# Scores of ten head pairs from q and k in two float32r parts, epsilon carried by the rows past the keys, and a new order of work

## The chip, the cores and the metric

The kernel runs on one core of one Trainium2 chip. The metric is the device time of one execution in microseconds (us). The kernel before took 669.44 us, the median of three runs (669.27 to 671.44).

## The reference

Soft-capped attention over 4 batches of 12 heads, 448 positions, head size 64, then a two-layer MLP with squared ReLU:

```
scores = (q @ k^T) / sqrt(64)
scores = cap * tanh(scores / cap)                    # cap = 30
attn   = exp(scores - max); attn /= (sum(attn) + 1e-9)
x      = attn @ v          -> 1792 tokens x 768
h      = x @ w_in          # 768 x 2048, float64-wide words hold the weights
out    = relu(h)^2 @ w_out # 2048 x 768
```

## The kernel before

For a cap of at most 40 (here 30) a branch is taken that leaves out the maximum, since the capped scores can't overflow `exp`. All that follows is that branch.

**Attention.** Heads go in 24 pairs `p`, six pairs to a batch `b`. One pair's q and k, transposed, fill 128 partitions (64 for each head), the tile `qkraw` (`first` for pair 0). The keys come in four chunks of 112. For a chunk TensorE (PE) makes the scores of both heads with two float32 matmuls, one on partitions 0 to 63 and one on 64 to 127 (`qk`, L215, tile `s`, two buffers). ScalarE (ACT) applies tanh (L224) and exp (L253), tile `t`. VectorE (DVE) adds the four chunks (L265, tile `added`), reduces the 32x32 blocks (L346), and `whole_sum` folds the parts, adds epsilon and takes reciprocals (L353 to L360); `tr2` spreads them (L329). PE multiplies the chunks with v (`pv`, L284, tile `po`, column halves for the two heads). DVE scales that into `xf` (L334).

**Split operands.** The MLP matmuls use float32r, whose precision is lower than float32's, so each operand is held in two parts: hi is the value cast to float32r (L164 on ACT or L166 on DVE), lo is value minus hi (L169, DVE). Of the four products three are made: `mm` in `unit`, L455 to L457, one each per 128x128 block of weights. There are 768 such triples; tile `f` (`ff` late) accumulates.

**Weights.** The 34 weight pieces arrive as 64-bit words (`raw`) and are rebuilt as float32 by `convert` (`mag` L393 or L395, `u` L405, L408, L411), split into `w` hi and lo (L164 or L166, then L169), used for batch 0, and stored to `k_in` and `k_out`; the later batches load them from there. After an `up` unit ReLU (L474 or L476), square (L479) and the split (L164 or L166, L169) make `g`; after a `down` unit L505 copies the result out.

**Order.** Each engine works through its instructions strictly in program order. That order is made when the program is built: a `Step` is a piece of work on one engine with a key (its intended place), an assumed duration, dependencies and buffers. A list scheduler plays the steps through in simulated time, taking on each engine the ready step with the lowest key, and a step that may run on ACT or DVE (`COPY`, `EITHER`) goes to whichever takes it first, with a penalty per engine (`GH` for `g` hi). So durations and penalties change the order and the engine of every later step.

Of the kernel before, what the change touches and what calls it, by code (L numbers as in the profile page):

```python
# [19 lines left out]
def tile_body(  # L20
# [25 lines left out]
    XH, GH, WH = 0.0, -2.0, 0.0  # L46
# [4 lines left out]
    if bounded:  # L51
        NBLK, NT = 34, 10
        EARLY, LAT, ADD_FROM = 4, 14, 0
        EXP, SUM, NORM = 2, 8, 12
        PSTEP = [4, 4, 4, 4]
# [22 lines left out]
    for i in range(4):  # L78
        par = i % 2
        v32[par].append(const.tile([CP, NCH, 2 * D], F32, name=f"v32_{i}"))  # L80
        if not bounded:
            nc.vector.memset(v32[par][-1][:, :, D:2 * D] if par == 0 else v32[par][-1][:, :, 0:D], 1.0)
# [6 lines left out]
    if bounded:  # L89
        nc.scalar.activation(out=eps, in_=capa, func=AF.Exp, scale=-1.0)  # L90
        nc.vector.tensor_scalar_mul(eps, eps, 1e-9)
        added = [const.tile([P, 2, S], F32, name=f"added{i}") for i in range(2)]
        for a in added:
            nc.vector.memset(a[96:P], 0.0)
    else:
        nc.vector.memset(eps, 1e-9)
# [15 lines left out]
        "o": ("hlf", [P, S], F32, 2, 0), "u": ("blk", None, U32, 2, 4), "mag": ("blk", None, F32, 2, 4),  # L112
        "first": ("free", None, None, 1, 0), "v0": ("free", None, None, 2, 0), "v1": ("free", None, None, 2, 0),
# [27 lines left out]
    class Step:  # L141
        def __init__(self, key, eng, dur, fn, deps=(), new=(), use=(), lag=0.15, behind=None, mode="full", port=False, calls=False):
            self.calls = calls
# [27 lines left out]
    def COPY(n, act=0.0, dve=0.0):  # L171
        return (
            {"ACT": 0.1 + n * 0.00085, "DVE": 0.07 + n * 0.00055},
            {"ACT": act, "DVE": dve},
        )

    def EITHER(act, dve):
        return {"ACT": act, "DVE": dve}, {"ACT": 0.0, "DVE": 0.0}

    def SUB(n):  # L180
        return 0.07 + n * 0.00105
# [5 lines left out]
    def heads(p, T, n_at):  # L187
# [12 lines left out]
        def load_v():  # L200
            for i in range(2):
                nc.sync.dma_start(out=vs[i].ap[:, :, i * D:(i + 1) * D], in_=v[b, :, h + i])

        ready = Step(T - 16, "SP", 1.5 * (p > 0), load, new=[raw], lag=3.0)
        got_v = Step(T, "SP", 1.4, load_v, new=vs, lag=3.0)

        tanhs = []
        for c0 in range(0, NCH, n_at):

            def qk(c0=c0):  # L210
                for c in range(c0, c0 + n_at):
# [8 lines left out]
            q = Step(T + (2 if b == 0 else QD) * c0, "PE", 0.75 * n_at, qk, [ready], new=s[cs] + t[cs], use=[raw], mode="rows")  # L220
            for c in range(c0, c0 + n_at):
# [4 lines left out]
                tanhs.append(Step(T + 2 * c + 1, "ACT", 0.9, tanh, [q], use=[s[c], t[c]]))  # L226

        if not bounded:
            a = tanhs[0]
            for c in range(1, NCH):  # L230

                def top(c=c):
# [3 lines left out]
                    T + 2 * c + 3, "DVE", 1.01, top, [a, tanhs[c]], calls=c == NCH - 1,  # L236
# [10 lines left out]
        for c in range(NCH):  # L247
# [8 lines left out]
            if not bounded:  # L256
                z = Step(T + 14 + 2 * c, "DVE", 1.01, less, [a], use=[t[c], ma], port=True)
            exps.append(Step(T + EXP + 2 * c, "ACT", 0.95, exp, [z], use=[t[c]]))

        if n_add:  # L260
            ts = Buf("ts")
            for c in range(1, NCH):

                def add(c=c):
# [4 lines left out]
                        T + EXP + 1 + 2 * c, "DVE", 1.01, add, exps[c - 1:c + 1] + adds,  # L269
# [5 lines left out]
        rows = [slice(0, D), slice(D, 2 * D)]  # L275

        by_ones = not bounded
        acc = [po, ss] if by_ones else [po]

        def pv(c0, n):  # L280
            def go():
                for c in range(c0, c0 + n):
                    for i in range(2):
                        nc.tensor.matmul(  # L284
                            po.ap[rows[i], 0:S], vs[i].ap[:, c, rows[i]], t[c].ap[:, i], start=c == 0, stop=c == NCH - 1
# [8 lines left out]
        def ones(u, start, stop):  # L294
            for i in range(2):
                nc.tensor.matmul(
                    ss.ap[rows[i], 0:S], vs[i].ap[:, 0, rows[1 - i]], u.ap[:, i], start=start, stop=stop
# [24 lines left out]
        def tr1():  # L322
            nc.vector.transpose(out=tr.ap, in_=sm.ap)
# [27 lines left out]
        def whole_sum():  # L351
# [4 lines left out]
            nc.vector.scalar_tensor_tensor(  # L356
                out=r[0:32], in0=z[0:32], scalar=eps[0:32], in1=o[0:32], op0=ALU.add, op1=ALU.add
            )
            for i in range(4):
                nc.vector.reciprocal(out=rc.ap[32 * i:32 * i + 32], in_=r[0:32, i // 2 * NB:(i // 2 + 1) * NB])  # L360

        T += NORM
        if by_ones:
            a = Step(T, None, EITHER(0.63, 0.56), sums, pvs[-1:], new=[sm], use=[ss])
            a = Step(T + 1, "DVE", 0.57, tr1, [a], new=[tr], use=[sm])
            a = Step(T + 1, "DVE", 0.17, rec, [a], new=[rc], use=[tr])
            a = Step(T + 1, "DVE", 0.56, tr2, [a], use=[rc, sm])
        else:
            a = Step(T, "DVE", 1.0, parts, adds, new=[q], use=[ts])
            a = Step(T, "DVE", 1.0, whole_sum, [a], new=[rc], use=[q])  # L370
            a = Step(T, "DVE", 0.64, tr2, [a], new=[sm], use=[rc])
        a = Step(T + 1, "DVE", 0.54, mult, [a] + pvs[-1:], new=[xf], use=[sm, po])
# [5 lines left out]
    def convert(T, src, dst, n):  # L378
# [47 lines left out]
        m = Step(T, None, EITHER(0.91 * d, 0.83 * d), rebase, [a], new=[mag], use=[raw])  # L426
        a = Step(T, "DVE", 0.02 + 0.48 * d, sign, [a], new=[u], use=[raw], port=True)
        a = Step(T, "DVE", 0.02 + 0.48 * d, low, [a], use=[raw, u], port=True)
        a = Step(T, "DVE", 0.07 + 0.8 * d, whole, [a, m], use=[u, mag], port=True)
# [35 lines left out]
    def up(T, d, b, m):  # L465
# [22 lines left out]
        a = Step(T, None, EITHER(0.54, 0.56), relu, done, new=[r], use=[hp])  # L488
        a = Step(T, "ACT", 0.53, square, [a], use=[r])
# [4 lines left out]
    def down(T, d, b, dm, q, acc):  # L494
# [15 lines left out]
        a = Step(T + d, "ACT", 0.46, evac, done, new=[o], use=[acc])  # L510
# [46 lines left out]
    while n_left:  # L557
        moved = False
        for e, q in ready.items():
# [15 lines left out]
            while q:  # L575
# [13 lines left out]
                if fit:  # L589
# [8 lines left out]
                    if e == "PE" and st.mode != mode:  # L598
                        dur += 0.15
# [98 lines left out]
```

## Time and profile before

| | |
|---|---|
| runs | 669.27, 669.44, 671.44 us |
| profiled execution | 670.38 us |
| its span in the profile | 668.6 us |
| PE, matmuls | 3072 records, busy 97% of the span |
| DVE, ACT busy | 332.4 and 333.5 us, 50% each |
| mean granted TensorE clock | 0.989 of full speed |

A float32 matmul leaves two records, one for each of its passes, a float32r matmul one. A PE record's length includes the pipeline, so records overlap; what a matmul costs is the distance from its start to the next start. Idle time in square brackets stands before the instruction, with what ended it.

### The profile page before, as it was taken

How to read it: one execution, taken by the hardware profiler on the slowest of the kernel's cores; microseconds unless marked ns; L12 is line 12 of the kernel's file. 1: busy time of each engine (PE TensorE's matmuls, PEld its weight loads, DVE VectorE, ACT ScalarE, POOL GpSimd, SP SyncE). 2: the span in 40 equal slices, each digit the busy share in tenths (PEclk: the TensorE clock that was granted, in tenths of full speed). 3: DMA queues.
4: the chain of work that ended last, by engine and by line, in shares of the span. 5: the costliest groups of instructions: out<-in, count | busy, mean ns of one | idle time of the engine just before them, and what ended most of it. 6: DMA issues, size and time to landing. Idle time of an engine off the chain costs nothing.

```text
span 668.6 us, 8034 instructions
## 1 busy us (share of the span) xinstructions
PE 646.4 (97%) x3072; PEld 486.2 (73%) x3072; DVE 332.4 (50%) x613; ACT 333.5 (50%) x456; POOL 0.2 (0%) x4
## 2 busy tenths in 40 slices
PE   4899998999999999999999999999999999999996
PEld 1234477667767798776798676767689999999996
DVE  3999999999999921565203146564620001110000
ACT  5899748677486425587202336858610005452000
POOL 0000000000000000000000000000000000000000
PEclk9799998999999999999999999999999999999999
DMA  8964587988899989864677576544348686666750
GB/s 204 301 181 131 154 264 269 331 283 273 297 311 333 336 286 335 236 181 137 191 239 235 182 235 184 166 156 140 97 156 262 223 280 227 222 187 205 257 162 31
DMA packets 57310, 148.46 MB, mean 222 GB/s; under 512 B 26288, under 2 KB 35504, under 8 KB 57264
## 3 DMA queue, kind: packets, MB, share of 16 engines
q1 hardware_dynamic: 57120, 147.64, 69.1%
q8 instruction: 26, 0.43, 0.3%
q10 hardware_dynamic: 144, 0.23, 0.1%
q14 instruction: 20, 0.16, 0.1%
HBM read 117.18 MB, written 30.67 MB: 221 GB/s over the span
## 4 chain that ended last, share of the span: by engine, by line
PE 88%; DVE 7%; DMA 2%; SPq 1%; issue 1%; ACT 1%; DVEq 0%
PE f L455 18%; PE f L457 17%; PE f L456 17%; PE s L215 10%; PE po L284 10%; PE ff L457 5%; PE ff L456 5%; PE ff L455 5%; DMA raw<-in_w_in_dram 2%; DVE added L265 1%; DVE u L411 1%; DVE w L169 1%; DVE rc L360 1%; DVE q L346 1%; DVE u L405 0%
## 5 line engine op out<-in xcount | busy, mean ns | idle before, releaser
L169 DVE TENSOR_TENSOR g<-r,g 128x448 fp32r<-128x448 f32 x64 | 39.6, 621 | 159.1 <-ACT g L164 158.9
L455 PE MATMUL f<-x,w 128*128 128x448 f32 x300 | 115.2, 384 | 3.0 <-DVE w L169 2.3
L457 PE MATMUL f<-x,w 128*128 128x448 f32 x300 | 110.5, 368 | 0.8 <-DVE x L169 0.7
L456 PE MATMUL f<-x,w 128*128 128x448 f32 x300 | 110.2, 367 | 0.0
L455 PE MATMUL f<-g,w 128*128 128x448 f32 x288 | 106.9, 371 | 0.5 <-DVE w L169 0.5
L457 PE MATMUL f<-g,w 128*128 128x448 f32 x288 | 105.2, 365 | 0.0
L456 PE MATMUL f<-g,w 128*128 128x448 f32 x288 | 105.2, 365 | 0.0
L224 ACT ACTIVATE t<-s,c 112x896 f32<-112x896 f32 x96 | 92.1, 1000 | 14.7 <-PE s L215 14.6
L253 ACT ACTIVATE t<-t,capa 112x896 f32<-112x896 f32 x96 | 96.3, 1039 | 0.2
L215 PE MATMUL s<-qkraw 64*112 64x448 f32 x368 | 83.6, 572 | 6.6 <-ACT t L224 6.6
L455 PEld LDWEIGHTS f<-x,w 128*128 128x128 f32 x300 | 56.7, 189 | 37.5 <-issue 24.4
L284 PE MATMUL po<-t,v 112*64 112x448 f32 x384 | 80.2, 561 | 0.0
L265 DVE TENSOR_TENSOR added<-added,t 112x896 f32<-112x896 f32 x48 | 52.1, 1085 | 48.7 <-ACT t L253 47.8
L455 PEld LDWEIGHTS f<-g,w 128*128 128x128 f32 x288 | 54.1, 188 | 14.5 <-issue 9.5
L457 PEld LDWEIGHTS f<-x,w 128*128 128x128 f32 x300 | 56.8, 189 | 6.4 <-DVE x L169 1.6
L505 ACT ACTIVATE o<-f 128x448 f32<-128x448 f32 x18 | 9.8, 545 | 102.8 <-PE f L457 102.8
L215 PEld LDWEIGHTS s<-qkraw 64*112 64x112 f32 x368 | 29.3, 174 | 43.2 <-issue 25.5
L456 PEld LDWEIGHTS f<-x,w 128*128 128x128 f32 x300 | 56.8, 189 | 3.9
L284 PEld LDWEIGHTS po<-t,v 112*64 112x64 f32 x384 | 26.1, 141 | 45.8 <-issue 42.1
L457 PEld LDWEIGHTS f<-g,w 128*128 128x128 f32 x288 | 54.1, 188 | 4.5
L456 PEld LDWEIGHTS f<-g,w 128*128 128x128 f32 x288 | 54.1, 188 | 4.2
L474 ACT ACTIVATE r<-f 128x448 f32<-128x448 f32 x42 | 22.7, 542 | 48.2 <-PE f L457 47.6
(52 smaller groups left out, 698.4 us busy)
## 6 DMA issues: line engine op xcount, KB each, us to landing
w<-k_in SPq DMA_DIRECT2D x48, 768.0 KB, 4.9
w<-k_out SPq DMA_DIRECT2D x36, 640.0 KB, 4.0
w<-k_out SPq DMA_DIRECT2D x18, 768.0 KB, 4.7
raw<-in_w_in_dram SPq DMA_DIRECT2D x16, 768.0 KB, 6.1
k_in<-w SPq DMA_DIRECT2D x16, 768.0 KB, 4.0
qkraw<-in_qkT_dram SPq DMA_DIRECT2D x46, 224.0 KB, 5.5
raw<-in_w_out_dram SPq DMA_DIRECT2D x12, 640.0 KB, 6.2
k_out<-w SPq DMA_DIRECT2D x12, 640.0 KB, 3.9
```

Source lines behind the costliest of these rows:

```text
L169: nc.vector.tensor_tensor(out=out, in0=in0, in1=in1, op=ALU.subtract)
L215: nc.tensor.matmul(s[c].ap[0:CP, i, 0:S], raw.ap[r, 1, ks], raw.ap[r, 0], start=True, stop=True)
L224: nc.scalar.activation(out=t[c].ap, in_=s[c].ap[0:CP, :, 0:S], func=AF.Tanh, scale=c1[0:CP])
L253: nc.scalar.activation(out=t[c].ap, in_=t[c].ap, func=AF.Exp, scale=capa[0:CP])
L265: nc.vector.tensor_tensor(out=ts.ap[0:CP], in0=t[0].ap if c == 1 else ts.ap[0:CP], in1=t[c].ap, op=ALU.add)
L284: nc.tensor.matmul(po.ap[rows[i], 0:S], vs[i].ap[:, c, rows[i]], t[c].ap[:, i], start=c == 0, stop=c == NCH - 1)
L346: nc.vector.tensor_reduce(out=q.ap[:, 0], in_=ts.ap.rearrange("p i (j c) -> p (i j) c", c=32), axis=mybir.AxisListType.X, op=ALU.add, appl ...
L455: nc.tensor.matmul(o, w.ap[:, 1, j], x[:, 0], start=first and j == 0, stop=False)
L456: nc.tensor.matmul(o, w.ap[:, 0, j], x[:, 0], start=False, stop=False)
L457: nc.tensor.matmul(o, w.ap[:, 0, j], x[:, 1], start=False, stop=last and j == n - 1)
L474: nc.scalar.activation(out=r.ap, in_=hp.ap[:, 0:S], func=AF.Relu)
L505: nc.scalar.activation(out=o.ap, in_=acc.ap[:, 0:S], func=AF.Copy)
```

## The change

The scores of pairs 14 to 23 (the last ten) are made from split operands. Per head, DVE or ACT casts q and k to float32r into partitions of a tile `m`, and a second cast writes k hi again into the other 64 partitions; DVE writes q lo beside it there, and k lo into a tile `lo`. One float32r matmul over all 128 partitions then makes (k hi)(q hi) + (k hi)(q lo), and a second one over 64 partitions adds (k lo)(q hi). The rows past the 112 keys of `added`, zero before, hold epsilon/16 each, so the sum has epsilon in it already; `whole_sum` then folds onto 64 partitions and takes two reciprocals in place of four. The tiles of ones that only the other branch reads are now filled in both, and all the fills stand on GpSimd (POOL). The planner's durations are replaced throughout, the penalty of `g` hi on DVE becomes 30.

```diff
-    XH, GH, WH = 0.0, -2.0, 0.0
+    SPLIT, SPT, ONES = B * H, -6.0, B * H
+    XH, GH, WH, EH = 0.0, 30.0, 0.0, 0.0
...
+        SPLIT, ONES = 14, 0
...
-        v32[par].append(const.tile([CP, NCH, 2 * D], F32, name=f"v32_{i}"))
-        if not bounded:
-            nc.vector.memset(v32[par][-1][:, :, D:2 * D] if par == 0 else v32[par][-1][:, :, 0:D], 1.0)
+        v32[par].append(const.tile([P, NCH, 2 * D], F32, name=f"v32_{i}"))
+        nc.gpsimd.memset(v32[par][-1][:, :, D:2 * D] if par == 0 else v32[par][-1][:, :, 0:D], 1.0)
...
         for a in added:
-            nc.vector.memset(a[96:P], 0.0)
+            nc.gpsimd.memset(a[96:P], 1.0 / (P - CP))
+            nc.gpsimd.tensor_scalar_mul(a[96:P], a[96:P], eps[96:P])
...
+                a = Step(T + SPT, None, COPY(896), hi, [ready], new=[m[i]] + [lo] * (i == 0), use=[raw])
+                operands += [
+                    Step(T + SPT + 1, None, COPY(448), k_hi, [ready, a], use=[raw, m[i]]),
+                    Step(T + SPT + 1, "DVE", 0.62, q_lo, [a], use=[raw, m[i]], port=True),
+                    Step(T + SPT + 1, "DVE", 0.62, k_lo, [a], use=[raw, m[i], lo], port=True),
+                ]
...
+                        nc.tensor.matmul(
+                            s[c].ap[0:CP, i, 0:S], m[i].ap[:, 1, ks], m[i].ap[:, 0], start=True, stop=False
+                        )
...
+                        nc.tensor.matmul(
+                            s[c].ap[0:CP, i, 0:S], lo.ap[rows[i], ks], m[i].ap[rows[i], 0], start=False, stop=True
+                        )
...
-            q = Step(T + (2 if b == 0 else QD) * c0, "PE", 0.75 * n_at, qk, [ready], new=s[cs] + t[cs], use=[raw], mode="rows")
+            q = Step(T + (2 if b == 0 else QD) * c0, "PE", (0.595 if split else 0.75) * n_at, qk, operands, new=s[cs] + t[cs], use=used, mode="rows", turn=0.0 if split else 0.19)
...
-            nc.vector.scalar_tensor_tensor(
-                out=r[0:32], in0=z[0:32], scalar=eps[0:32], in1=o[0:32], op0=ALU.add, op1=ALU.add
-            )
-            for i in range(4):
-                nc.vector.reciprocal(out=rc.ap[32 * i:32 * i + 32], in_=r[0:32, i // 2 * NB:(i // 2 + 1) * NB])
+            nc.vector.tensor_copy(o[32:64], z[0:32])
+            nc.vector.tensor_tensor(out=r[0:64], in0=z[0:64], in1=o[0:64], op=ALU.add)
+            for i in range(2):
+                nc.vector.reciprocal(out=rc.ap[rows[i]], in_=r[0:64, i * NB:(i + 1) * NB])
...
-        a = Step(T, None, COPY(448, dve=XH), x_hi, [a], new=[x], use=[xf])
```

(The last two lines stand for the durations: some twenty steps get another number, most of them a larger one.)

PE, in the last batch but one, between two `up` units: two chunks of scores of one pair, before.

```order
L456 MATMUL f<-x,w 128x448
L457 MATMUL f<-x,w 128x448
L215 MATMUL s<-qkraw 112x448 x4
L455 MATMUL f<-x,w 128x448
L456 MATMUL f<-x,w 128x448
```

PE, the same step after the change (L245 is the matmul over 128 partitions, L251 the one over 64; L499 to L501 are the former L455 to L457).

```order
L500 MATMUL f<-x,w 128x448
L501 MATMUL f<-x,w 128x448
L245 MATMUL s<-m 112x448 x4
L251 MATMUL s<-m,lo 112x448 x4
L499 MATMUL f<-x,w 128x448
L500 MATMUL f<-x,w 128x448
```

Four float32 matmuls have become eight float32r ones, the four full-height ones first. This stands twice for each of the ten pairs.

DVE, the first sum of a pair (`q` holds partial sums, `rc` reciprocals), before.

```order
L353 COPY q<-q 64x28
L354 TENSOR_TENSOR q<-q 64x28
L355 COPY q<-q 32x28
L356 SCALAR_TENSOR_TENSOR q<-q,eps 32x28
L360 RECIPROCAL rc<-q 32x14 x4
```

DVE, the same sum after the change.

```order
L395 COPY q<-q 64x28
L396 TENSOR_TENSOR q<-q 64x28
L397 COPY q<-q 32x28
L398 COPY q<-q 32x28
L399 TENSOR_TENSOR q<-q 64x28
L401 RECIPROCAL rc<-q 64x14 x2
```

Eight instructions have become seven; this stands 24 times.

DVE at the start of the program, before.

```order
L94 MEMSET added_141 32x896
L94 MEMSET added_142 32x896
L84 TENSOR_SCALAR capn<-capb 128x1
L85 TENSOR_TENSOR capa<-capb,capn 128x1
L86 RECIPROCAL rcap<-capa 128x1
L87 TENSOR_SCALAR c_128<-rcap 128x1
L91 TENSOR_SCALAR eps<-eps 128x1
L265 TENSOR_TENSOR added_141<-t 112x896
L405 TENSOR_SCALAR u<-raw 128x768
```

DVE at the start after the change.

```order
L88 TENSOR_SCALAR c_128<-rcap 128x1
L92 TENSOR_SCALAR eps<-eps 128x1
L439 TENSOR_SCALAR mag<-raw 128x768
L449 TENSOR_SCALAR u<-raw 128x768
L308 TENSOR_TENSOR added_145<-t 112x896
L452 TENSOR_SCALAR u<-raw 128x768
```

POOL at the start after the change; L308 on DVE waits for the first of its two multiplies. Before, POOL had none of these rows.

```order
L83 MEMSET v_0_130 128x4x64
L83 MEMSET v_1_132 128x4x64
L83 MEMSET v_2_134 128x4x64
L83 MEMSET v_3_136 128x4x64
L96 MEMSET added_145 32x896
L96 MEMSET added_146 32x896
L97 ISA
L97 TENSOR_SCALAR added_145<-added_145,eps 32x896
L97 TENSOR_SCALAR added_146<-added_146,eps 32x896
```

The two fills have left DVE, the first add now stands behind two conversion steps and has a new wait for POOL. L97 ISA is an instruction that the build puts ahead of POOL's first multiply and that loads POOL's library of code.

## Rows read from the trace of the kernel before

**Rows 1.** The page's first part: busy us, share, instructions.

```profile
PE 646.4 (97%) x3072; PEld 486.2 (73%) x3072; DVE 332.4 (50%) x613; ACT 333.5 (50%) x456; POOL 0.2 (0%) x4
```

**Rows 2.** Windows: us, busy by engine (x records), granted clock, DMA share, GB/s.

```profile
60.00:80.00 20.00, 18.60 (x86) 7.65 (x84) 19.43 (x39) 15.05 (x18) 0.00 (x0) 1.00 0.53 141
...
100.00:120.00 20.00, 17.67 (x78) 14.56 (x77) 19.27 (x31) 16.79 (x24) 0.00 (x0) 0.91 0.79 275
120.00:140.00 20.00, 20.00 (x97) 14.02 (x96) 19.70 (x37) 15.48 (x23) 0.00 (x0) 1.00 0.89 331
...
160.00:180.00 20.00, 20.00 (x99) 15.61 (x99) 18.84 (x35) 7.11 (x10) 0.00 (x0) 1.00 0.95 309
...
460.00:480.00 20.00, 20.00 (x96) 13.05 (x96) 11.43 (x22) 14.37 (x21) 0.00 (x0) 1.00 0.43 138
```

**Rows 3.** Timeline of PE around two chunks of scores: start, length, what.

```profile
399.82 0.37 PE L456 MATMUL f<-x,w 128*128 128x448 f32 x1
400.03 0.36 PE L457 MATMUL f<-x,w 128*128 128x448 f32 x1
400.32 1.76 PE L215 MATMUL s<-qkraw 64*112 64x448 f32 x8
402.01 0.47 PE L455 MATMUL f<-x,w 128*128 128x448 f32 x1
402.32 0.36 PE L456 MATMUL f<-x,w 128*128 128x448 f32 x1
```

**Rows 4.** Timeline of PE's weight loads in the same block.

```profile
400.32 0.28 PEld L215 LDWEIGHTS s<-qkraw 64*112 64x112 f32 x4 [0.31 <-issue]
400.79 0.18 PEld L215 LDWEIGHTS s<-qkraw 64*112 64x112 f32 x2 [0.20 <-issue]
```

**Rows 5.** Timeline of PE, up to 105 us: stations and waits.

```profile
36.93 0.47 PE L455 MATMUL f<-x,w 128*128 128x448 f32 x1
...
73.37 3.23 PE L284 MATMUL po<-t,v 112*64 112x448 f32 x16
76.53 0.47 PE L455 MATMUL f<-x,w 128*128 128x448 f32 x1
...
77.31 0.47 PE L457 MATMUL f<-x,w 128*128 128x448 f32 x1
...
80.01 0.47 PE L455 MATMUL f<-x,w 128*128 128x448 f32 x1
...
100.72 0.37 PE L457 MATMUL f<-x,w 128*128 128x448 f32 x1
103.41 0.47 PE L455 MATMUL f<-x,w 128*128 128x448 f32 x1 [2.33 <-DVE w L169]
```

**Rows 6.** Timeline of DVE: what the waits at 77 and 103 us are for.

```profile
76.64 0.62 DVE L169 TENSOR_TENSOR x<-xf,x 128x448 fp32r<-128x448 f32 x1
...
102.41 0.95 DVE L169 TENSOR_TENSOR w<-u,w 128x768 fp32r<-128x768 f32 x1
```

**Rows 7.** Groups of DVE instructions by shape: busy, mean ns of one, idle before.

```profile
L360 DVE RECIPROCAL rc<-q 32x14 f32<-32x14 f32 x96 | 22.2, 231 | 2.7
...
L356 DVE SCALAR_TENSOR_TENSOR q<-q,eps 32x28 f32<-32x28 f32 x24 | 5.6, 235 | 0.8
...
L355 DVE COPY q<-q 32x28 f32<-32x28 f32 x24 | 4.0, 168 | 0.8
...
L166 DVE CAST w<-u 128x768 fp32r<-128x768 f32 x8 | 4.4, 548 | 0.2
...
L169 DVE TENSOR_TENSOR x<-xf,x 128x448 fp32r<-128x448 f32 x24 | 14.9, 621 | 6.5 <-ACT x L164 6.5
```

**Rows 8.** Timeline of DVE at the start.

```profile
2.68 1.75 DVE L94 MEMSET added<- 32x896 f32 x2 [2.68 <-issue]
...
8.46 0.15 DVE L91 TENSOR_SCALAR eps<-eps 128x1 f32<-128x1 f32 x1 [1.23 <-ACT eps L90]
...
13.40 0.61 DVE L405 TENSOR_SCALAR u<-raw 128x768 uint16<-128x768 uint16 x1 [0.20 <-DMA raw<-in_w_in_dram]
```

## What the change was predicted to do

> **What bounds the kernel now.** The page's first part comes first: PE is busy 97% of the span, DVE and ACT 50% each [rows 1]. That share is a mean over stages, so the windows come next. From 120 us on the windows hold 96 to 99 matmul records and PE is busy in all of it, while DVE falls from 19.7 busy us of 20 to 11.4 [rows 2]. So from 120 us PE's own work sets the pace, and only less of that work, or cheaper work, makes this part shorter. Earlier it is another matter: PE has 86 records in 60:80 and 78 in 100:120, and there DVE is busy for 19.4 and 19.3 us of 20 [rows 2]. DVE is the bound up to about 110 us and PE waits for what it makes.
>
> PE's timeline gives its prices. Float32r matmuls start 0.203 us apart (399.82 to 400.03 is 0.21; 99 in 20 us, with hardly a score block among them, are 0.202) [rows 2, 3]. Two chunks of float32 scores lie between the starts at 400.03 and 402.32, where without them one matmul would start and the next follow: 2.29 - 2 x 0.203 = 1.88 us [rows 3]. Four twos of records at 0.375 make 1.50 of that (two twos, 0.75, for a chunk); 0.38 is the change of array shape, 0.09 going in (400.03 to 400.32), 0.19 before the next matmul at 402.01, 0.10 after it.
>
> The waits up to 110 us that matter: at 77.31, where 0.51 us after 76.53 was due, 0.27 us for x lo of DVE (at 76.64, 0.62 long) [rows 5, 6]; at 103.41, 2.69 - 0.20 = 2.49 us for a weight's lo part, which DVE ended at 103.36 [rows 5, 6]. Behind that wait the granted clock is 0.91 in the window of 20 us [rows 2]: it is 1.00 in the windows on either side, so about 3.6 us ran at the lower of its two levels (1.2 for 2.4 GHz), which costs 1.8 us.
>
> **The change part by part.**
>
> *Scores in two parts.* Twenty blocks of two chunks (ten pairs) change. Each loses 1.88 us. It gains four matmuls of full height, which follow the MLP's without a change of shape: 4 x 0.203 = 0.81. Then come four of 64 rows, in two pairs. The float32 matmuls of the two heads run side by side: their weight loads come in twos that take 0.18 us together, a two every 0.38 us [rows 4], and eight records fit in 1.50 us. If float32r pairs share likewise, two pairs take 2 x 0.19 to 0.203, taken as 0.39. The change of shape now stands between the full matmuls and the pairs, 0.38 as before. Sum 1.58, a gain of 0.30 a block, 20 x 0.30 = **-5.9 us**. No row shows float32r on 64 rows. Bounds: with the change of shape free the block takes 1.20, a gain of 13.6; with the pairs one after the other it takes 0.81 + 0.81 + 0.38 = 2.00, a loss of 2.4. I take the middle, because the nearest rows, those of the same heads on the same halves, show both the sharing and the price of the switch.
>
> The Trainium skill ("TensorEngine Tiling (Array Packing)", Key Properties) says that a change of tiling mode drains TensorE. By that rule the switch is paid once in and once out of each block, as in my sum; the planner's new price of the block, which has no cost on the way in, would give 20 x 0.2 = 4 us more gain. The trace agrees with the rule: 0.38 us around each block.
>
> *The operands of those scores.* In the new order DVE gets 15 casts of 64x896, 14 of 64x448 and 40 subtractions, ACT 5 and 6 casts. A cast of 768 elements takes 548 ns and a subtraction of 448 takes 621 ns [rows 7]; with 0.62 for 896 and 0.39 for 448 elements DVE gets 9.3 + 5.5 + 24.8 = 40 us, ACT some 8. All of it lies in 240 to 480 us, where DVE is busy 11 us in 20 and ACT 14 in a loaded window [rows 2]: over twelve windows 40 us is 3.3 each. It is hidden; the first operands stand in the order more than twenty DVE instructions ahead of their matmuls. Without that cover a pair would cost its 5 us. The queues behind are ACT's and DVE's `g` steps, which PE needs only a unit later.
>
> *The sums.* Each loses four reciprocals and a fused add, 4 x 0.231 + 0.235 = 1.16 us, and gains a copy, an add of the same size, taken as long, and two reciprocals, 2 x 0.168 + 2 x 0.231 = 0.80 [rows 7]: -0.36 us of DVE for each pair. From 240 us this is off the path; before, it is part of the next term.
>
> *The new order up to 110 us.* DVE is the bound there, so I count what stands ahead of two of its results in both orders, with the durations of the trace. Ahead of the sixth pair's x lo: 69.5 us before, 62.6 now (six sums -2.1, fills -1.6, two casts less and one more left to ACT -1.3, a weight's last two steps now behind it -1.9). The fills ran at 2.68, behind idle time and long before the first conversion at 13.40, so they give nothing back [rows 8]: -5.3 remains. In the start the two orders draw level: DVE now waits for `raw` at 13.4 [rows 8], but then has no more gaps until its first reduction. So x lo is there at 77.26 - 5.3 = 72.0. PE's matmuls for it began at 76.53 and were held at 77.31 [rows 5]. PE itself comes there in time: its first MLP matmul, at 36.93 before [rows 5], has one chunk (0.75) less ahead of it, and from it to these the new list holds 18 chunks of scores, 16 of `pv` at the same 0.75, 30 MLP matmuls and some 20 edges at 0.19: 36.2 + 13.5 + 12.0 + 6.1 + 3.7 = 71.5. So they end near 73.0. Then comes one `pv` block, now ahead, 73.37 to 76.53 or 3.16 [rows 5], and the first long run of MLP matmuls, at 80.01 before [rows 5], starts at 76.2. One score block of 1.88 that stood before it now stands behind: 80.0 - 76.2 - 1.9 = **-1.9 us**.
>
> Ahead of the eighth weight's lo part, the one missed at 103.41, stand 97.6 us before and 86.5 now; less the fills that is -9.5, so it is there at 93.9, while PE asks for it at 76.2 + 2 x 7.5 + 1.9 + 3.4 + 3.7 = 100. The wait of 2.49 and the slow clock behind it, 1.8, go, and some 0.1 of small ones: **-4.4 us**. Of the few waits after 120 I claim nothing. What is late next is again a weight, with a margin of 6 us here and about 2 in the list up to 135 us. Runs and edges of blocks differ by one, +0.1.
>
> *The epsilon rows.* The first add on DVE now waits for POOL: four fills, two more, the library load and a multiply by eps, which is there at 8.61 [rows 8]. That add is due at 14.4, behind two conversion steps of some 0.5 that wait for `raw` at 13.4 [rows 8]. No row shows POOL at such work. By DVE's pace for a fill (0.8 us) [rows 8] POOL is done by about 10 us, cost nothing; at three times that pace it would end near 20 and hold DVE by 5, plus the load. I take nothing, by the nearest row; that is the least known cost. Behind the add stands all of DVE.
>
> **Sum.** -5.9 - 1.9 - 4.4 + 0.1 = -12.1 us. From the profiled execution's own 670.38 us that is **658.3 us**; the median before is 0.9 lower, 669.44, and the tail after the last matmul is unchanged.
>
> **The rivals.**
>
> 1. *The 64-row matmuls don't share their time.* Then each block costs 2.00 us: +8.1 on the forecast, 666.4. For it: no row of float32r on half the rows. Against it: the two heads' weight loads in the score block come in twos, 0.18 us for two [rows 4], so the halves work side by side. Chance 0.10.
>
> 2. *A weight load waits for the stream on its own rows.* Within a block the second pair of 64-row matmuls uses the same halves as the first. If its load can't be hidden, each block takes another 0.17: +3.4, 661.7. Against it: at the block's start four loads fit in 0.28 us, so the second two went in while the first stream ran [rows 4]. The Trainium skill ("TensorE: Matmul & The Clock Gate", Part 3) says that loads overlap running matmuls only when the row group differs, and would have this rival; the trace differs, and decides. Chance 0.08.
>
> 3. *The supply comes no sooner.* DMA is busy 0.89 to 0.95 between 120 and 180 us [rows 2]; if weights and not DVE set that pace, or the planner's new list has gaps of its own, the 6.3 us of the early part stay: 664.6. Against it: the waits that the trace names are for DVE [rows 5]. Chance 0.15.
>
> 4. *POOL holds DVE, and the kernel gets slower.* Place: the first add at 14.4 us. Price: 1 us of delay there shifts every x and weight, and PE has only the 6 us of margin at the eighth weight and 2 further on, so a delay comes through nearly whole: 658.3 plus the delay. From 11 us on (POOL done at 25) it is no gain, from 13 on clearly slower; at 20 it is 678. For it: the library load, of unknown length. Against it: eight short instructions in the 11 us from 2.7 on. Chance 0.12, of which 0.10 over the point.
>
> **Chances and range.** The forecast has 0.55, with 655 to 661 as its own range. What a measurement of this kernel can tell from no change is about 0.3%, 2 us. Faster: the forecast, rivals 2 and 3, most of rival 1 and a little of 4, 0.82; within 0.3%: 0.07; slower: 0.11. Low end: the switch free (-4) and the last waits gone as well (-3), 651. High end: rival 1 with part of rival 3, 668.
>
> **What would show it.** Blocks of scores in pairs 14 to 23 near 1.6 us between MLP matmuls, eight records; 1.2 or 2.0 would show the bounds. The first long MLP run near 76 us in place of 80, no wait of over 1 us and no fall of the clock between 80 and 120. DVE's first add not waiting for POOL. PE busy without a gap in 240 to 480 although DVE has 3 us more in each window. The forecast is wrong if PE waits for DVE or ACT after 120 us, or if POOL's multiply ends after 14.4.

## The result, and the profile after

The kernel after takes 662.82 us, the median of four runs (662.46 to 663.41), beside 669.67 us before: 0.9893 of it, 95% interval 0.9874 to 0.9913. That is 6.9 us less; the forecast of 658.3 would be 11.4 less. The profiled execution took 662.46 us, its span is 660.6.

The page's first part and the windows of [rows 2], now for the kernel after, with one added at 220 us. Columns as there: busy us of PE, PEld, DVE, ACT, POOL with the number of records, granted clock, DMA share, GB/s.

```profile
PE 639.6 (97%) x3072; PEld 493.9 (75%) x3072; DVE 355.2 (54%) x647; ACT 345.2 (52%) x476; POOL 8.0 (1%) x12
```

```profile
60.00:80.00 20.00, 18.58 (x89) 9.55 (x86) 19.47 (x39) 19.68 (x26) 0.00 (x0) 1.00 0.63 197
100.00:120.00 20.00, 20.00 (x98) 15.82 (x98) 17.61 (x33) 15.37 (x23) 0.00 (x0) 1.00 0.89 290
120.00:140.00 20.00, 20.00 (x96) 13.09 (x97) 18.24 (x32) 16.29 (x25) 0.00 (x0) 1.00 0.85 296
160.00:180.00 20.00, 20.00 (x97) 13.03 (x96) 18.55 (x33) 11.52 (x15) 0.00 (x0) 1.00 0.86 298
220.00:240.00 20.00, 17.37 (x72) 14.92 (x71) 15.94 (x31) 5.53 (x8) 0.00 (x0) 0.83 0.93 316
460.00:480.00 20.00, 20.00 (x100) 15.81 (x99) 12.49 (x26) 12.61 (x19) 0.00 (x0) 1.00 0.36 118
```

Against [rows 2] the window 100:120 has 98 records for 78 and the full clock for 0.91: the wait at 103 us is gone. The window 220:240 is the new bad one: 72 records, clock 0.83, where the kernel before, shown here, has 98 and 1.00:

```profile
220.00:240.00 20.00, 20.00 (x98) 15.08 (x97) 16.54 (x30) 8.51 (x11) 0.00 (x0) 1.00 0.91 321
```

In the kernel after DVE is below 19 us of 20 from 100 us on, though it has more to do in all (355.2 us for 332.4); in [rows 2] it is at 19.7 in 120:140.

PE's timeline shows one split block, the start of the first long MLP run, and the stall. Columns: start, length, what, idle time before and what ended it.

```profile
75.81 0.47 PE L499 MATMUL f<-x,w 128*128 128x448 f32 x1
...
220.67 0.37 PE L501 MATMUL f<-g,w 128*128 128x448 f32 x1
223.00 0.47 PE L499 MATMUL f<-g,w 128*128 128x448 f32 x1 [1.96 <-DVE w L173]
...
224.54 0.57 PE L499 MATMUL f<-g,w 128*128 128x448 f32 x1
224.91 0.57 PE L500 MATMUL f<-g,w 128*128 128x448 f32 x1
225.28 0.57 PE L501 MATMUL f<-g,w 128*128 128x448 f32 x1
226.53 0.74 PE L499 MATMUL f<-g,w 128*128 128x448 f32 x1 [0.67 <-DVE w L173]
...
242.61 0.97 PE L245 MATMUL s<-m 128*112 128x448 f32 x4
243.51 0.67 PE L251 MATMUL s<-m,lo 64*112 64x448 f32 x4
244.11 0.48 PE L499 MATMUL f<-x,w 128*128 128x448 f32 x1
244.42 0.37 PE L500 MATMUL f<-x,w 128*128 128x448 f32 x1
```

- **Block.** From 242.61 to 244.11 is 1.50, and the next two starts are 0.31 apart in place of 0.20: 1.60 us, for 1.88 in [rows 3]. All twenty blocks take 1.50 (median). 20 x 0.28 = 5.6 us.
- **Early part.** The first long run starts at 75.81, for 80.01 in [rows 5].
- **Stall.** After 220.67 PE should go on at 220.88 and goes on at 223.00. Behind it matmuls start 0.37 us apart (224.54, 224.91, 225.28): half the clock. The run of 93 matmuls from 217.68 on takes 24.94 us; at 0.203 each with its edges it is 19.0. So this place costs 5.9 us, 2.6 in the two waits and 3.3 at the lower clock:

```profile
218.00:224.00 6.00, 4.04 (x20) 3.37 (x19) 6.00 (x11) 2.22 (x4) 0.00 (x0) 1.00 0.94 245
224.00:231.00 7.00, 6.33 (x18) 5.10 (x17) 6.69 (x16) 2.31 (x3) 0.00 (x0) 0.51 1.01 414
231.00:238.00 7.00, 7.00 (x37) 6.44 (x36) 5.25 (x9) 2.38 (x4) 0.00 (x0) 1.00 0.80 240
```

These are windows of the kernel after, in which DVE is busy without a gap up to 224 and PE has 18 records in 7 us at a clock of 0.51. What PE waits for at 223.00 is a weight's lo part. DVE's timeline ahead of it (kernel after):

```profile
215.10 1.05 DVE L308 TENSOR_TENSOR added<-added,t 112x896 f32<-112x896 f32 x1
216.79 0.83 DVE L173 TENSOR_TENSOR w<-u,w 128x640 fp32r<-128x640 f32 x1 [0.64 <-ACT w L168]
217.53 0.62 DVE L376 TENSOR_TENSOR xf<-po,sm 128x448 f32<-128x448 f32 x1
...
221.61 0.60 DVE L173 TENSOR_TENSOR x<-xf,x 128x448 fp32r<-128x448 f32 x1
222.14 0.81 DVE L173 TENSOR_TENSOR w<-u,w 128x640 fp32r<-128x640 f32 x1
...
223.74 1.09 DVE L388 TRANSPOSE_TENSOR_REDUCE q<-added 128x28 f32<-128x896 f32 x1
224.87 0.62 DVE L173 TENSOR_TENSOR m<-qkraw,m 64x448 fp32r<-64x448 f32 x1
225.52 0.96 DVE L173 TENSOR_TENSOR w<-u,w 128x768 fp32r<-128x768 f32 x1
```

What matters is what stands among the weights' steps: adds, `xf` and `x` of a pair that PE wants only in the third pass (its first matmul on `x` starts at 384.6 us), a reduction of the next pair, and a subtraction for the first split scores. DVE also waits there for ACT's hi casts. Its waits from 110 to 222 us, in the kernel after (us in total, times, longest):

```profile
DVE w L173 <- ACT w L168: 6.1, 6, 1.5
DVE u L449 <- DMA raw<-in_w_out_dram: 1.7, 1, 1.7
```

Before, the first of these is 0.3 us in one wait.

The profile's sum is: split blocks -5.6; start of the first long run -4.2, of which 1.9 is a score block that only changed sides, so -2.3; the wait at 103 with its slow clock -4.2; small delays of before at 80 to 235 us, about -1.8 by the distances of starts (the other terms leave -1.7 for them); the stall +5.9. That is -8.0, and the two profiled executions differ by 670.38 - 662.46 = 7.9.

### The profile page after: what moved, and what is told of

It reads as the page before. It is cut to its first block, busy times and chain, and to the rows that moved or that the text cites. A ratio compares the mean times of both kernels' runs of the same rounds, so it can differ in the third digit from the quotient of the medians.

```text
span 660.6 us, 8078 instructions
## 1 busy us (share of the span) xinstructions
PE 639.6 (97%) x3072; PEld 493.9 (75%) x3072; DVE 355.2 (54%) x647; ACT 345.2 (52%) x476; POOL 8.0 (1%) x12
## 4 chain that ended last, share of the span: by engine, by line
PE 88%; DVE 6%; ACT 2%; issue 1%; DMA 1%; SPq 1%; DVEq 0%
PE f L499 19%; PE f L501 18%; PE f L500 18%; PE po L325 9%; PE ff L501 6%; PE ff L500 6%; PE ff L499 6%; PE s L258 4%; PE s L245 2%; DVE added L308 2%; PE s L251 2%; DMA raw<-in_w_in_dram 1%; ACT t L267 1%; ACT t L296 1%; DVE u L455 1%
## 5 line engine op out<-in xcount | busy, mean ns | idle before, releaser
L499 PE MATMUL f<-x,w 128*128 128x448 f32 x300 | 114.6, 382 | 0.8 <-ACT x L168 0.5
L499 PE MATMUL f<-g,w 128*128 128x448 f32 x288 | 108.2, 376 | 2.6 <-DVE w L173 2.6
L501 PE MATMUL f<-x,w 128*128 128x448 f32 x300 | 109.9, 366 | 0.6 <-DVE x L173 0.6
L500 PE MATMUL f<-g,w 128*128 128x448 f32 x288 | 106.3, 369 | 0.0
L501 PE MATMUL f<-g,w 128*128 128x448 f32 x288 | 106.3, 369 | 0.0
L499 PEld LDWEIGHTS f<-x,w 128*128 128x128 f32 x300 | 56.4, 188 | 29.1 <-issue 20.0
L325 PE MATMUL po<-t,v 112*64 112x448 f32 x384 | 78.0, 545 | 0.0
L499 PEld LDWEIGHTS f<-g,w 128*128 128x128 f32 x288 | 54.8, 190 | 17.7 <-issue 9.1
L308 DVE TENSOR_TENSOR added<-added,t 112x896 f32<-112x896 f32 x48 | 51.9, 1081 | 28.7 <-ACT t L296 28.1
L501 PEld LDWEIGHTS f<-x,w 128*128 128x128 f32 x300 | 56.5, 188 | 5.7 <-DVE x L173 1.0
L501 PEld LDWEIGHTS f<-g,w 128*128 128x128 f32 x288 | 54.8, 190 | 4.5
L500 PEld LDWEIGHTS f<-g,w 128*128 128x128 f32 x288 | 54.8, 190 | 4.2
L258 PE MATMUL s<-qkraw 64*112 64x448 f32 x208 | 47.9, 573 | 6.9 <-ACT t L267 6.9
L376 DVE TENSOR_TENSOR xf<-po,sm 128x448 f32<-128x448 f32 x24 | 14.8, 616 | 54.7 <-PE po L325 54.1
```

The source lines that it names most:

```text
L258: nc.tensor.matmul(s[c].ap[0:CP, i, 0:S], raw.ap[r, 1, ks], raw.ap[r, 0], start=True, stop=True)
L308: nc.vector.tensor_tensor(out=ts.ap[0:CP], in0=t[0].ap if c == 1 else ts.ap[0:CP], in1=t[c].ap, op=ALU.add)
L325: nc.tensor.matmul(po.ap[rows[i], 0:S], vs[i].ap[0:CP, c, rows[i]], t[c].ap[:, i], start=c == 0, stop=c == NCH - 1)
L376: nc.vector.tensor_tensor(out=xf.ap, in0=po.ap[:, 0:S], in1=sm.ap, op=ALU.mult)
L499: nc.tensor.matmul(o, w.ap[:, 1, j], x[:, 0], start=first and j == 0, stop=False)
L500: nc.tensor.matmul(o, w.ap[:, 0, j], x[:, 0], start=False, stop=False)
```

## The experiments

Times are medians; ratios are to the kernel before, run beside each group. The group of `after_again` measured the kernel after at 0.989 once more.

| kernel | us | ratio, interval |
|---|---|---|
| b_split | 664.49 | 0.9921 [0.9902, 0.9940] |
| b_sum | 665.64 | 0.9935 [0.9918, 0.9952] |
| b_both | 660.46 | 0.9851 [0.9833, 0.9868] |
| a_oldsum | 665.45 | 0.9934 [0.9918, 0.9951] |
| a_whi | 661.03 | 0.9875 [0.9854, 0.9896] |
| a_late | 660.50 | 0.9864 [0.9843, 0.9885] |
| a_chain | 666.00 | 0.9934 [0.9919, 0.9948] |
| a_defer | 667.77 | 0.9962 [0.9948, 0.9977] |
| after_again | 662.53 | 0.9890 [0.9865, 0.9915] |
| a_best1 | 658.65 | 0.9831 [0.9804, 0.9858] |
| a_best2 | 661.05 | 0.9867 [0.9842, 0.9892] |
| b_best | 661.41 | 0.9865 [0.9839, 0.9891] |

### Which part of the change gives what

**b_split**: the split scores alone, in the order of before.

```diff
+        SPLIT = 14
...
```

(The steps `hi`, `k_hi`, `q_lo`, `k_lo` and the new `qk` follow, as in the change.)

> The kernel before, with one part of the change: the last ten pairs' scores in two parts, the order rebuilt with the old durations and equal to that of before up to about 300 us. Theory (a block of two chunks falls from 1.88 to 1.60 us, twenty of them): 0.28 x 20 = 5.6 us less than before, 0.9917 of its time, with the waits of before at 77, 103, 167, 181 and 233 us still there. Rival (the gain of the change lies in its order and sums, and the split blocks give nothing because their operands' casts hold TensorE): within 0.3% of before.

5.3 us less; all blocks 1.50 as in the kernel after. The operands' casts cost nothing that shows beside an interval of 0.2% on each side.

**b_sum**: the new sums and the epsilon rows alone.

```diff
...
-            for i in range(4):
-                nc.vector.reciprocal(out=rc.ap[32 * i:32 * i + 32], ...)
+            nc.vector.tensor_copy(o[32:64], z[0:32])
+            nc.vector.tensor_tensor(out=r[0:64], in0=z[0:64], in1=o[0:64], op=ALU.add)
+            for i in range(2):
+                nc.vector.reciprocal(out=rc.ap[rows[i]], in_=r[0:64, i * NB:(i + 1) * NB])
```

> The kernel before in its own order, with the new sums (two reciprocals on 64 rows, a copy and an add for four reciprocals and a fused add) and the epsilon rows filled by GpSimd. Theory of the prediction's supply steps, as far as the durations alone make them: DVE does six times 0.36 us less ahead of the sixth pair's x lo and some 0.36 x 7 ahead of the eighth weight, so the wait of 2.49 us at 103 us falls below 0.5 and with it the slow clock behind it (1.8): 3 to 5 us less than before. Rival (the order made the early gain, the sums alone none): within 0.3% of before, with the wait at 103 us still over 1.5 us.

4.4 us less, as the theory has it. One step of it is off: the wait at 100 us is shorter but still there. PE's row, and its window, for [rows 5] and [rows 2]:

```profile
100.63 0.47 PE L455 MATMUL f<-x,w 128*128 128x448 f32 x1 [1.52 <-DVE w L170]
```

```profile
100.00:120.00 20.00, 19.37 (x94) 14.60 (x95) 19.81 (x31) 19.06 (x30) 0.00 (x0) 1.00 0.91 313
```

The wait lost 0.8 of 2.33 us, and the slow clock behind it went: 1.00 for 0.91. That the shorter wait kept the clock up is not shown: in b_split's profiled execution the wait at 102 us is 2.34 us, as in the kernel before, and the window 100:120 has 1.00 too. The first long run starts at 78.29 us for 80.01 before, by the sums alone.

**b_both**: both of these, still planned with the durations of before, and so in its order up to about 300 us.

> The kernel before with the new sums, the epsilon rows on GpSimd and the split scores, but planned with the old durations (the order of before up to about 300 us). Theory (the new sums give 4.2 us, the split scores 5.4 us, they add up, and the new order of the whole change costs some 2.5 us by its stall at 220 us): 669.9 - 9.6 = 660.2 us, 2 to 3 us less than after, no wait for a weight at 220 us, the clock at 1.00 in all windows from 120 us on. Rival (the order of after is better or neutral, and the parts do not add up): 662 to 664 us.

660.46 us: the parts add up (0.9921 x 0.9935 = 0.9857 for 0.9851), and this kernel has no wait for a weight at 220 us. It is 2.3 us below the kernel after (its four runs 659.77 to 662.18, the ten of the kernel after 661.0 to 664.1). So the new order, the third part of the change, does not help here; by the two ratios it costs 0.4%, with intervals of 0.2% on each side. The two kernels were not run in one group, and their profiled executions are only 0.3 us apart (662.18, the slowest of b_both's four, and 662.46). Where the new order costs shows in the supply: DVE's lo parts of the weights that PE waits for in the kernel after, at 222.14 and 225.52 us there, start in b_both at

```profile
218.34 0.83 DVE L173 TENSOR_TENSOR w<-u,w 128x640 fp32r<-128x640 f32 x1 [0.34 <-ACT w L168]
221.78 0.96 DVE L173 TENSOR_TENSOR w<-u,w 128x768 fp32r<-128x768 f32 x1
```

They come 3.7 to 3.8 us sooner, while PE reaches them later: by 217 us it has begun 216 score and 208 `pv` records, for 224 and 222 in the kernel after, with as many MLP matmuls (497 and 498).

**a_oldsum**: the reverse, the order of after with the old sums and fills.

```diff
...
+            nc.vector.memset(a[96:P], 0.0)
...
-            nc.vector.tensor_copy(o[32:64], z[0:32])
-            nc.vector.tensor_tensor(out=r[0:64], in0=z[0:64], in1=o[0:64], op=ALU.add)
...
+            nc.vector.scalar_tensor_tensor(out=r[0:32], in0=z[0:32], scalar=eps[0:32], in1=o[0:32], ...)
...
```

> The kernel after in its own order, with the old sums (four reciprocals and a fused add) and the old zero fills on DVE. Theory (DVE's work ahead of x and of the weights is the bound up to 240 us, and the order alone gives nothing): each pair's sum puts 0.36 us back on DVE, six of them ahead of the first long MLP run (2 us) and thirteen ahead of the 31st weight (4.7 us, of which its idle time takes some): 3 to 7 us more than after. Rival (the new order made the early gain, the sums do not matter): within 0.3% of after.

2.6 us more than after, just under the low end of the 3 to 7 expected. The first long run starts at 79.66 for 75.81: the order alone, without the new sums and fills, stands where before stood (80.01), although one score block fewer lies ahead of the run. Not all of these 3.8 us are DVE's work. The granted clock fell ahead of the run, behind waits of 0.73 and 1.30 us, to 0.88 in the window 66:80, where after has 1.00; that is about 1.7 us. The run of 93 takes 23.8 for 24.9, though PE waits longer in it (1.97, 1.44 and 0.62 us): here the clock stayed at 1.00. The first of these waits, as long as the one in after:

```profile
226.70 0.47 PE L499 MATMUL f<-g,w 128*128 128x448 f32 x1 [1.97 <-DVE w L172]
```

### What makes the stall at 220 us

**a_whi**: six hi casts of weights go from ACT to DVE.

```diff
+        for n in (11, 15, 19, 21, 27, 29):
+            w_his[n].eng = "DVE"
```

> The kernel after in its own order, but six of the weights' hi casts (those at which DVE waited for ACT between 115 and 217 us, 6.1 us in all) are made by DVE itself. Theory 1 (ACT's late casts make DVE idle, and this idle time ate the lead of the weights): six casts of 0.55 us are added to DVE and 6.1 us of idle time go, so the 31st weight is there 2 to 3 us sooner, the waits of 1.96 and 0.67 us at 221 and 225 us shrink below 1 in all and the clock stays up: 3 to 6 us less than after. Theory 2 (the casts and subtractions of the first pair with split scores, at 207 to 225 us, hold back the last weights): within 0.3% of after. Theory 3 (DVE has simply too much work ahead of the last weights, idle or not): the added 3.3 us make it the same or up to 3 us longer.

**a_late**: the split operands behind the last weight.

```diff
+        early = [st for st in ISSUE[:end] if st.fn.__name__ in ("hi", "k_hi", "q_lo", "k_lo")]
+        ISSUE = [st for st in ISSUE[:end] if st not in early] + early + ISSUE[end:]
```

> The kernel after, but the operand steps of the split scores that stood ahead of the last weight's lo part in the order (casts on ACT and DVE, subtractions on DVE, from 207 us on) come right behind it. Theory 2 (these steps hold back the last weights): DVE has some 2 us less ahead of the 31st to 33rd weight, and ACT 4.6 us less ahead of their hi casts, so the waits at 221 and 225 us shrink to under 1 us in all and the clock stays up: 4 to 6 us less than after. Theory 1 (ACT's late hi casts between 115 and 202 us ate the lead): the stall stays over 1.5 us with the slow clock behind it, 0 to 2 us less than after. If the operands come too late for their first scores, a new wait near 240 us shows it.

Each comes out near 2 us below after, which is no more than these intervals tell (0.9875 and 0.9864 for 0.9893, each with 0.2% on either side); neither theory has its full gain. PE's waits in the stretch, first a_whi, then a_late:

```profile
221.69 0.47 PE L499 MATMUL f<-g,w 128*128 128x448 f32 x1 [1.20 <-DVE w L173]
225.22 0.47 PE L499 MATMUL f<-g,w 128*128 128x448 f32 x1 [1.44 <-DVE w L173]
230.58 0.47 PE L499 MATMUL f<-g,w 128*128 128x448 f32 x1 [0.23 <-DVE w L173]
```

```profile
222.03 0.47 PE L499 MATMUL f<-g,w 128*128 128x448 f32 x1 [1.28 <-DVE w L173]
224.82 0.47 PE L499 MATMUL f<-g,w 128*128 128x448 f32 x1 [0.70 <-DVE w L173]
230.43 0.47 PE L499 MATMUL f<-g,w 128*128 128x448 f32 x1 [0.48 <-DVE w L173]
```

The waits add up to as much as in after (2.9 and 2.5 us for 2.6), but the longest fell from 1.96 to 1.44 and 1.28, and the window 220:240 has the clock at 1.00 in both. What these executions gained is the slow clock, not the waits. That the moves kept the clock up is not shown: in a_oldsum it stayed up behind longer waits.

**a_chain** moves DVE's non-urgent sums and x parts behind the last weight; **a_defer** those and the operands.

```diff
+        early = [st for st in ISSUE[sums:end] if st.fn.__name__ in ("parts", "whole_sum", "tr2", "mult", "x_hi", "x_lo")]
+        ISSUE = [st for st in ISSUE[:end] if st not in early] + early + ISSUE[end:]
```

> The kernel after, but the reductions, sums, transposes, products and x parts of the two pairs whose x is wanted only in the third pass (near 385 us), which stood among the last weights from 210 us on, come right behind the last weight's lo part. Nothing else is moved; a part of the split operands stays where it was. Theory 3 (DVE's work ahead of the last weights is the bound there, and part of it is not urgent): ahead of the weight that PE waits for at 221 us DVE has 4.3 us less (1.1 + 1.6 + 0.64 + 0.53 + 0.53), more for the next; the waits of 1.96 and 0.67 us go, the clock stays at 1.00, 5 to 6 us less than after, 657 us. Theory 1 (ACT's late hi casts hold DVE there whatever it has to do): DVE is idle instead, the stall stays over 1.5 us, 0 to 3 us less than after. A third way (the raw weights' transfers are late): DVE waits for raw, the same.

> The kernel after with both moves: the two pairs' sums and x parts and the operand steps of the first split scores all stand behind the last weight's lo part. Theory 3: no wait at 220 us, as without the second move, so nothing more to gain: 657 us, 5 to 6 us less than after, unless the split operands now come too late for the scores at 236 us, which would show as a wait of 1 to 3 us there. Theory 2 (the operand steps are what matters): 2 us less than the kernel that moves the sums alone.

Both miss: some 3 and 5 us slower than after. About 2 us of that are not from the moves. In the profiled executions the first long run starts at 77.89 (a_chain) and 77.57 us (a_defer) for 75.81, though nothing differs from the kernel after up to 205 us: behind two waits of about 1 us at 67 and 69 us the clock fell. The window 66:80 of a_chain, then of after:

```profile
66.00:80.00 14.00, 12.04 (x49) 6.12 (x47) 12.89 (x26) 12.11 (x18) 0.00 (x0) 0.88 0.48 160
66.00:80.00 14.00, 12.84 (x61) 7.58 (x58) 13.74 (x27) 13.71 (x19) 0.00 (x0) 1.00 0.67 203
```

after_again has two waits of the same length there (0.98 and 0.94 us) and kept 1.00.

In a_chain the run of 93 falls only to 22.9 us, because DVE, with less to do, waits for ACT (first row, DVE), and the delayed steps push out a subtraction for the split scores (second row, PE):

```profile
218.71 0.82 DVE L173 TENSOR_TENSOR w<-u,w 128x640 fp32r<-128x640 f32 x1 [3.21 <-ACT w L168]
```

```profile
245.54 0.66 PE L245 MATMUL s<-m 128*112 128x448 f32 x2 [2.72 <-DVE m L173]
```

In a_defer the run falls to 21.1 us, and PE's waits in it to 1.2 us in all, for 2.9 in a_chain and 2.5 in a_late: the two moves shorten the waits only together. But the wait for the split scores at 245 us grows to 4.73 us: two subtractions of the first split pair stood originally behind the last weight, and the moved sums now stood ahead of them. The moves were right and the place was wrong.

**a_best1** puts the sums behind all operands of that pair.

```diff
+        ISSUE = [... not in moved ...] + ops + late + [... not in moved ...]
```

> The kernel after with the operand steps of the first split pair behind the last weight's lo part, and only behind all of them the sums and x parts of the two pairs whose x is wanted in the third pass; their x hi cast goes from ACT to DVE. Theory (the two moves took 3.9 of the 5.9 us off the run of 93 matmuls, and what they gave back came from the two subtractions of a score operand that stood behind the moved sums): the run takes 21.0 us, no wait at 240 us, 4 us less than after, about 659 us. Rival (DVE's late sums hold a relu, a tanh's add or the next operands at 245 to 260 us): a new wait of 1 to 5 us there and no gain.

658.65 us, as expected: all five runs (657.56 to 660.41) lie below the six of after on the same chip (661.04 to 664.09). There is no wait at 240 us, the run of 93 takes 21.0 us for 24.9 (1.6 us less of waits, the rest mostly the slow clock that did not come), and the window to hold against that of after is:

```profile
220.00:240.00 20.00, 18.93 (x92) 15.82 (x90) 15.32 (x28) 7.95 (x12) 0.00 (x0) 1.00 0.98 378
```

It beats both kernels, but cannot be told from b_both (0.9831 and 0.9851). So the cause of the stall is shown: work that is wanted later stood ahead of the last weights' steps, on DVE (sums, x, subtractions) and on ACT (operand casts, x hi casts). How much each of them held is not told apart. What remains are 2 us.

**a_best2** adds the six hi casts on DVE.

```diff
+        for n in (11, 15, 19, 21, 27, 29):
+            w_his[n].eng = "DVE"
```

> The same, and the six hi casts of weights at which DVE waited for ACT are made by DVE. Theory 1 (ACT's hi casts are what is left at 218 to 224 us, where DVE still waited 1.5 and 0.96 us for them): the run of 93 falls by another 1 us to some 20 us, 658 us. Rival (the raw weights' transfers are what is left: DMA share 1.00 in 220 to 240, ACT and DVE waited for raw there 0.8 to 1.8 us at a time): the run stays at 21.0 us, the same time as without.

Neither: 2.4 us more than a_best1 (five runs each, 660.78 to 661.77 for 657.56 to 660.41). DVE's hi casts did end sooner, but then the raw weight behind them is what is late. DVE's row for it, a_best1 and then a_best2:

```profile
223.99 0.54 DVE L449 TENSOR_SCALAR u<-raw 128x640 uint16<-128x640 uint16 x1 [0.80 <-DMA raw<-in_w_out_dram]
```

```profile
225.54 0.55 DVE L449 TENSOR_SCALAR u<-raw 128x640 uint16<-128x640 uint16 x1 [2.94 <-DMA raw<-in_w_out_dram]
```

SP's queue shows where that load comes from, again a_best1 and then a_best2:

```profile
217.56 0.87 SPq L206 DMA_DIRECT2D v<-in_v_dram  x2
218.47 1.19 SPq L428 DMA_DIRECT2D raw<-in_w_out_dram  x2
```

```profile
218.30 1.09 SPq L206 DMA_DIRECT2D v<-in_v_dram  x2
219.45 0.95 SPq L428 DMA_DIRECT2D raw<-in_w_out_dram  x2
```

The last two raw loads stand in SP's order behind the loads of the next pair's `v`, whose buffers PE's `pv` block gives back only when it ends: in the waits of SP's queue the `v` loads waited for `po` 1.5 us in a_best1 and 3.1 us in a_best2. The transfer then runs at a DMA share of 0.98 to 1.00. So the rival's bound is there, the supply of raw; but that the six casts themselves brought the other 2 us is not shown, since PE also reached this place 0.7 us later, by waits in the first 40 us, where the two kernels are the same program. Raw loads ahead of `v` in SP's order were not tried.

**b_best** moves one sum in the order of before.

```diff
+        late = [ISSUE[sums], ISSUE[at("whole_sum", 7)]]
+        ISSUE = [st for st in ISSUE[:end] if st not in late] + late + ISSUE[end:]
```

> The kernel before with new sums and split scores (old durations and order), and one step moved: the reduction and sum of the eighth pair (2.7 us of DVE, wanted only in the second pass, near 240 us) stand behind the lo part of the weight that PE waits for at 102 us, not ahead of it. ACT is idle for 5 us there and waits for DVE, so DVE alone is the bound: theory: that lo part comes 2.7 us sooner, the wait of 1.6 us goes, 1.6 to 2 us less than without the move, 0.9825 of before, about 658.5 us. Rival (the weight behind it is as late, or raw's transfers are the bound): the wait stays over 1 us or moves to the next weight, no gain.

The rival holds: the wait of b_both at 102 us goes, and the next weight's lo part, which now has the sum ahead of it, is waited for. PE's row and window:

```profile
110.72 0.50 PE L496 MATMUL f<-x,w 128*128 128x448 f32 x1 [1.78 <-DVE w L173]
```

```profile
100.00:120.00 20.00, 18.22 (x82) 14.60 (x82) 19.59 (x35) 14.82 (x23) 0.00 (x0) 0.91 0.86 290
```

DVE is full there (19.6 of 20). A step put off by one weight makes the next late; in a_best1 it was put off past the last one, to where DVE has room (14 us of 20 in 240 to 260).

**after_again**, the kernel after beside the last three:

> The kernel after once more, unchanged, beside the versions that follow from the experiments. By all theories 0.989 of before, with the waits at 221 and 225 us and the fall of the clock behind them; if the early waits up to 80 us differ from the first profile's, this is the spread to hold against the other kernels.

The long wait is the same (1.97 us), the second is 0.33 for 0.67 us, and the clock fell for a shorter time: the run of 93 takes 23.4 us. Its six runs spread over 3 us with the mean granted clock between 0.990 and 0.997.

## Why the prediction was right, and which step failed

Forecast 658.3 us, measured 662.8: on the side forecast and in the range of 651 to 668, but outside the forecast's own 655 to 661. The gain is 0.6 of the one forecast.

- **Split scores, -5.9.** Right in mechanism and size: -5.6 by the blocks, -5.3 by b_split. The 64-row pairs share their time: from the first of the four to the next MLP matmul are 0.60 us. The price of the shape change is there too: the four full matmuls take 0.90 for 0.81, and 0.19 and 0.10 stand behind the pairs. Rivals 1 (2.00 a block) and 2 (1.75) are out, although rival 2's 661.7 us is the number nearest to the measured one. PE's weight loads in the block (kernel after) answer to [rows 4]:

```profile
242.41 0.78 PEld L245 LDWEIGHTS s<-m 128*112 128x112 f32 x4
243.51 0.27 PEld L251 LDWEIGHTS s<-m,lo 64*112 64x112 f32 x4 [0.32 <-issue]
```

  All four loads of the pairs, two to a half, are in 0.27 us after the first began, and their four matmuls take 0.60. The Trainium skill ("TensorE: Matmul & The Clock Gate", Part 3) says in its list of what overlaps that loads overlap running matmuls only on another row group (earlier in that part it also lets loads into the background weight buffer go ahead); this trace differs from the list, as [rows 4] did.
- **Operands at nothing.** Right after 240 us: PE is busy in all of 460:480 with DVE at 12.5. Wrong for the first split pair, whose steps fall among the last weights; a_late, which moves them out of the way, is about 2 us faster, no more than its interval tells, and by a_defer they count only together with the sums.
- **Early part, -1.9, and the wait at 103, -4.4.** Right in size: 75.81 for 76.2, no wait between 80 and 217 us, clock 1.00. The cause was misplaced in part. The working spread the gain over sums, fills, casts and weights' steps that moved; b_sum has 4.4 us without any move, and in a_oldsum, with all of the moves, the first long run is 3.8 us later, about 1.7 of it slow clock.
- **POOL at nothing.** Right, rival 4 is out, but the price behind it was not: the two multiplies by eps take 2.5 us each, three times the 0.8 us of DVE's fill. The margin covered it: they end at 12.7 us, one us before DVE's first add at 13.87, which does not wait. In POOL's timeline no load of code shows beside them, so what L97 ISA loads, and what that costs, is shown by no run:

```profile
3.45 1.63 POOL L96 MEMSET added<- 32x896 f32 x2
7.58 5.15 POOL L97 TENSOR_SCALAR added<-added,eps 32x896 f32<-32x896 f32 x2 [2.50 <-DVE eps L92]
```

- **What failed: "Of the few waits after 120 I claim nothing".** The step behind it, a margin of 6 us at the eighth weight and about 2 further on, was worked out to 135 us and left there. It had to be carried to the last weight. PE was 2.3 us ahead at the first long run and some 8 us at 217 us (the terms of the profile's sum above), while the new order put sums, x and operand steps between the last weights' steps, so that these came no sooner than before (lo parts done at 222.95 and 226.47 us, for 222.34 and 225.92). The lead was used up by 220 us, and the stall of 5.9 us there is more than the whole miss of 4.5 us; the small delays of before that went as well, for which the sum had nothing either, took 1.8 off again. The reading behind the step was off too: PE is not busy in all of the time from 120 us on in the kernel before, which has 94 records and 19.50 busy us in 180:200, with a wait of 0.51 us for a weight at 182.69. The prediction named PE waiting for DVE after 120 us as a sign of being wrong, and the sign came, but it had no place in the sum. Rival 3 (664.6) came near in size for another reason: the early gain is there, and most of it is given back at 220 us.
- **Two sums of the prediction.** With the switch free the block's bound gives 13.6 us, 7.7 more than the forecast, but the low end takes only 4 for it; by its own bound it would be about 647. Rival 1's 2.00 a block is 8.3 us over the forecast, not 8.1. Neither touches the forecast.

What stays open: why the granted clock fell in some of these waits and not in others. It fell behind single waits of 2.33 us (before), 1.96 and 1.97 (after, twice), 2.10 (a_best2) and 1.78 (b_best), and behind two of about 1 us close together (a_chain, a_defer). It did not fall behind 1.44 and 1.28 (a_whi, a_late), but neither behind 2.34 (b_split, 102 us), 1.97 (a_oldsum, 227 us), or the same two of about 1 us in after_again and a_best1. The length of a wait alone does not tell.

## What to carry to other kernels

When a pacing engine is relieved, follow the lead that its consumer gains down to the last item of the supply, engine by engine, not to the next two items. Ahead of the last items look for work that is wanted much later and put it behind all of them, and behind what else is due next; put off by one item, or ahead of other due work, it only moves the wait. Test an order apart from the operations: here the operations were worth 9.8 us in the old order, and the new order took some 2 to 3 of them back.

## What was not expected of the hardware

A multiply of 32x896 by a scalar takes GpSimd 2.5 us, for 0.8 us of a fill of the same size. A stall with a wait of under 2 us for PE cost 3.3 us more through the clock than its waits lasted (after), and a wait of the same length elsewhere cost nothing more (a_oldsum, 1.97 us). The kernel after took 661.0 to 664.1 us in ten runs; how much of that spread is the clock at this place was not measured.
